# One core, chunked attention into a gated MLP: a weight load in two, one half's transposes on another engine, and output banks turned by two

## The chip, the cores and the metric

The kernel runs on one core of a Trainium2 chip. The metric is the device time of that core in microseconds (us), median of several executions. TensorE is called PE, its weight loads PEld, VectorE DVE, ScalarE ACT, GpSimd POOL, and SP issues most of the loads and stores (156 of the 159 DMA issues in the profile of before). "L702" is line 702 of the kernel. In the changed kernel every line that matters here has a number higher by one (L702 became L703).

## The reference

Two stages. The first is attention inside chunks of 64 positions, the second an MLP with a gate on all 4608 tokens:

```python
# q, k, v: (8, 8, 576, 64), 9 chunks of 64 per sequence
scores = np.matmul(q_c, k_c.transpose(0, 1, 2, 4, 3)) / np.sqrt(64)
attn = np.exp(scores - scores.max(-1, keepdims=True))
attn = attn / (attn.sum(-1, keepdims=True) + 1e-09)
x = np.matmul(attn, v_c)              # rearranged to (4608, 512)
h = x @ w_in                          # w_in  (512, 2048)
g = h / (1.0 + np.exp(-beta * h))
out = g @ w_out                       # w_out (2048, 512)
```

All inputs and the output are float32.

## The kernel before

The tokens go through in 9 blocks of 512, each of two **halves** h (h = 0 to 17). For each half the kernel casts q and k to bf16, turns them (transposes), makes the scores, the exponentials, the average of v, and turns the result into xT. For each block, `mm1` makes 16 tiles of x @ w_in, `gate` makes g from each, and `mm2` makes out. The kernel gives PE eight buffers for its results, the **banks**; it lets a bank be written again when the engine that reads it is done (in the trace of before, PE stands 1.31 us for a gate that reads its bank). A Python list scheduler fixes the order on each engine when the program is built: where several pieces of work are ready, the one of lowest rank goes first, by cost estimates in us. Each engine is given its list; in the trace of before, DVE, waiting for one entry, holds up the ready ones behind it (it stands 1.98 us, and a gate is ready for the last 0.9 of them).

```python
A0, A1, A2, A3, F3, F0, F1, F2 = range(8)     # the eight PSUM banks
FS = (F0, F1, F2, F3)

def load_w_in(j, queue):                      # piece j: 512 of 2048 columns, 1 MB
    ...
    P.dma(queue, (0.65, 32, 79), lambda e: e.dma_start(
        stage, w_in[:, f0:f0 + n].rearrange("(c p) f -> p c f", p=128)), ...)

def turn_pe(h, which, j, m, n):               # on PE, into a bank; 8 transposes for q, 8 for k
    ...
def keep_turned(h, which, j, m, n, eng):      # the copy out of that bank, q on ACT, k on DVE
    ...
def turn_dve(h, which, hb):                   # on DVE, 32-bit stream transpose, from SBUF to SBUF
    ...
def scores(h, cps, b=A0, first=0.2):          # after turn_pe: 32 matmuls
    ...
def scores_halved(h, first=0.2):              # after turn_dve: 64 smaller matmuls
    ...
def gate(blk, t, n, halves=(0, 1)):           # the DVE part is the one that frees the bank
    P.op("act", ..., lambda e: e.activation(tt[:, T % 3, c], bank(n)[:, c], AF.Tanh, scale=beta_half[:, t:t + 1]), ...)
    P.op("dve", ..., lambda e: e.scalar_tensor_tensor(
        g2[:, sg, t, c], tt[:, T % 3, c], 1.0, bank(n)[:, c], ALU.add, ALU.mult), ...)
...
PAIRED = (3, 4, 5)                            # halves turned on DVE; 0 to 2 on PE, 6 and later by DMA
HOLD = {(5, 0, 0): (1, 1)}                    # a turn_dve of half 5 waits for a gate of block 1

def turn(h, banks=(A0, A1)):
    for w in (1, 0):
        if h >= 2 and h not in PAIRED:
            go(r, cast_qk, h, w, 0, 8, "pool")
            go(r, turn_pe, h, w, 0, 8, banks[w])
            go(URGE.get(h, 0), keep_turned, h, w, 0, 8, banks[w], ("act", "dve")[w])
            continue
        if h >= 2:
            go(r, cast_rows, h, w, "pool")
            for hb in range(2):
                go(TD.get(h, 2), turn_dve, h, w, hb, after=gated.get(HOLD.get((h, w, hb))))
            continue
        ...
...
for j in range(4):
    for s in range(4):                        # block 0, second product: banks F0 to F3
        go(200 + 10 * j + s, mm2, 0, s, range(4 * j, 4 * j + 4), FS[s])
...
for t in range(4, 16):                        # block 1, first product
    ...
    go(300 + 4 * t, mm1, 1, t, FS[t % 4], hvs)
    gated[1, t] = go(0, gate, 1, t, FS[t % 4], hvs)
...
for blk in range(2, NB):                      # blocks 2 to 8: mm1 beside mm2 of the block before
    ...
        n = FS[i % 2]                         # mm1 in F0, F1
        m = FS[2 + s % 2] if 2 * blk + 2 < FIRST else F2   # mm2 in F2, F3
```

The softmax here doesn't subtract the row's maximum and nothing guards it: scores larger than these inputs give would overflow.

## Time and profile before

| what | before |
|---|---|
| device time, median of 3 | 294.1 us (293.81 to 294.6) |
| span of the profiled run | 292.8 us |
| PE busy | 277.7 us (95%) |
| DVE, ACT, POOL busy | 157.8, 149.3, 103.0 us |
| DMA share, 4 to 74 us | 1.04 to 1.16 |

PE is the bound. The lines that carry this are in the prediction below. One row of the table of stretches belongs here. The columns are the stretch and its length in us, then for PE, PEld, DVE, ACT and POOL the busy us with the number of instructions, then the granted PE clock, the DMA share and GB/s:

```profile
46.00:60.00 14.00, 12.49 (x252) 7.38 (x254) 8.51 (x17) 8.08 (x15) 8.90 (x12) 1.00 1.09 297
```

PE is busy 12.49 of 14 us here.

A warning for reading this profile: it lacks 34 matmul records of L730 (x558), while all 592 of its weight loads are there. Small gaps on the matmul row of before, such as "L730 <- issue", are partly these holes.

### The profile page before, as it was taken

How to read it: one execution, taken by the hardware profiler on the slowest of the kernel's cores; microseconds unless marked ns; L12 is line 12 of the kernel's file. 1: busy time of each engine (PE TensorE's matmuls, PEld its weight loads, DVE VectorE, ACT ScalarE, POOL GpSimd, SP SyncE). 2: the span in 40 equal slices, each digit the busy share in tenths (PEclk: the TensorE clock that was granted, in tenths of full speed). 3: DMA queues.
4: the chain of work that ended last, by engine and by line, in shares of the span. 5: the costliest groups of instructions: out<-in, count | busy, mean ns of one | idle time of the engine just before them, and what ended most of it. 6: DMA issues, size and time to landing. Idle time of an engine off the chain costs nothing.

```text
span 292.8 us, 6026 instructions
## 1 busy us (share of the span) xinstructions
PE 277.7 (95%) x2534; PEld 138.3 (47%) x2568; DVE 157.8 (54%) x280; ACT 149.3 (51%) x226; POOL 103.0 (35%) x112
## 2 busy tenths in 40 slices
PE   1999999899999999999999999999999999999995
PEld 1774444544444444444444444444444444444444
DVE  1557974798365355465655565655555544334300
ACT  3569533576555544545555555555555454454311
POOL 1444756535786845433243565212120000000000
PEclk9979999999999999999999999999999999999999
DMA  7999999999999999999898979282824110101133
GB/s 200 298 386 401 280 392 263 303 296 247 202 262 210 229 245 187 271 217 234 214 256 214 241 209 262 61 183 52 185 50 128 36 72 0 74 8 63 54 87 77
DMA packets 91722, 55.97 MB, mean 191 GB/s; under 512 B 76712, under 2 KB 76976, under 8 KB 91696
## 3 DMA queue, kind: packets, MB, share of 16 engines
q1 hardware_dynamic: 91520, 55.46, 73.6%
q8 instruction: 20, 0.33, 0.5%
q10 hardware_dynamic: 176, 0.14, 0.2%
q14 instruction: 6, 0.05, 0.0%
HBM read 36.71 MB, written 9.44 MB: 158 GB/s over the span
## 4 chain that ended last, share of the span: by engine, by line
PE 77%; DMA 11%; SPq 4%; DVE 3%; issue 1%; ACT 1%; POOL 1%; ACTq 0%; POOLq 0%
PE A L730 37%; PE A L702 37%; DMA qkstage<-in_moe_w_out_dram 5%; DMA g<-in_moe_w_out_dram 3%; DMA qkstage<-in_k_dram 3%; SPq L417 2%; PE A L615 2%; DVE g L720 2%; SPq L452 2%; PE A L566 1%; DVE w_out_bf L349 1%; SPq L432 1%; ACT tt L717 1%; POOL w_out_bf L349 1%; DVE qkO L522 0%
## 5 line engine op out<-in xcount | busy, mean ns | idle before, releaser
L720 DVE SCALAR_TENSOR_TENSOR g<-tt,A 128x512 bf16<-128x512 bf16 x144 | 97.4, 685 | 92.1 <-ACT tt L717 91.2
L717 ACT ACTIVATE tt<-A,beta_half 128x512 bf16<-128x512 f32 x144 | 98.4, 687 | 94.4 <-PE A L702 91.4
L702 PE MATMUL A<-xT,w_in_bf 128*128 128x512 bf16 (+1 forms) x608 | 142.5, 371 | 1.6 <-DVE g L720 1.6
L730 PE MATMUL A<-w_out_bf,g 128*128 128x512 bf16 (+1 forms) x558 | 135.6, 373 | 2.9 <-issue 0.8
L702 PEld LDWEIGHTS A<-xT,w_in_bf 128*128 128x128 bf16 x608 | 58.0, 99 | 64.6 <-DVE g L720 7.1
L730 PEld LDWEIGHTS A<-w_out_bf,g 128*128 128x128 bf16 x592 | 56.8, 98 | 64.4 <-POOL w_out_bf L349 0.6
L349 POOL COPY qkO<-qkT 128x1024 bf16<-128x1024 bf16 x17 | 33.4, 1980 | 31.7 <-DMA qkT<-qkb 31.7
L349 POOL CAST qkb<-qkstage 128x1024 bf16<-128x1024 f32 (+1 forms) x30 | 30.7, 1022 | 36.8 <-DMA qkstage<-in_k_dram 26.5
L347 ACT ACTIVATE ostage<-A 128x512 f32<-128x512 f32 (+1 forms) x36 | 21.3, 591 | 20.2 <-PE A L730 20.2
L349 POOL CAST v_bf<-vstage 128x512 bf16<-128x512 f32 x32 | 19.6, 615 | 20.5 <-DMA vstage<-in_v_dram 20.0
L655 DVE TENSOR_TENSOR xn<-A,R 128x512 bf16<-128x512 f32 (+2 forms) x44 | 25.4, 593 | 1.2
L603 ACT ACTIVATE E<-A 128x1024 bf16<-128x1024 f32 (+1 forms) x18 | 15.5, 880 | 4.8 <-PE A L566 4.1
L349 DVE COPY qkO<-qkT 128x512 bf16<-128x512 bf16 x14 | 11.3, 849 | 0.2 <-DMA qkT<-qkb 0.2
L503 PE MATMUL A<-ident,qkb 128*128 128x128 bf16 x48 | 4.6, 251 | 6.1 <-DVE qkb L349 5.7
L615 PEld LDWEIGHTS A<-v_bf,E 64*64 64x64 bf16 x576 | 6.9, 107 | 7.1 <-issue 4.2
L522 DVE STREAM_TRANSPOSE qkO<-qkb 128x256 uint32<-128x256 uint32 x12 | 6.9, 644 | 5.4 <-POOL qkb L349 5.4
L615 PE MATMUL A<-v_bf,E 64*64 64x65 bf16 x576 | 9.8, 195 | 0.0
L660 DVE RECIPROCAL R<-A 128x8 f32<-128x8 f32 (+2 forms) x36 | 7.2, 199 | 4.3 <-PE A L615 4.3
L349 POOL CAST w_in_bf<-wstage 128x512 bf16<-128x512 f32 (+1 forms) x10 | 5.8, 616 | 7.3 <-DMA wstage<-in_moe_w_in_dram 7.3
L744 DVE TENSOR_SCALAR ostage<-A 128x256 f32<-128x256 f32 x1 | 0.4, 425 | 13.3 <-PE A L730 13.3
L349 POOL CAST qkb<-wstage 128x1024 bf16<-128x1024 f32 x4 | 4.5, 1136 | 8.0 <-DMA wstage<-in_k_dram 5.5
L566 PE MATMUL A<-qkO 64*64 64x64 bf16 x480 | 7.0, 197 | 0.1
(36 smaller groups left out, 72.8 us busy)
## 6 DMA issues: line engine op xcount, KB each, us to landing
qkstage<-in_k_dram SPq DMA_DIRECT2D x16, 512.0 KB, 4.7
qkstage<-in_q_dram SPq DMA_DIRECT2D x16, 512.0 KB, 5.7
vstage<-in_v_dram SPq DMA_DIRECT2D x32, 256.0 KB, 6.6
out_dram<-ostage SPq DMA_DIRECT2D x16, 512.0 KB, 4.3
wstage<-in_moe_w_in_dram SPq DMA_DIRECT2D x4, 1024.0 KB, 8.6
qkstage<-in_moe_w_out_dram SPq DMA_DIRECT2D x2, 1024.0 KB, 15.7
g<-in_moe_w_out_dram SPq DMA_DIRECT2D x2, 1024.0 KB, 8.1
wstage<-in_q_dram SPq DMA_DIRECT2D x8, 128.0 KB
```

The costliest lines, as they stand in the source:

```text
L347: P.op("act", us, lambda e: e.activation(dst, src, AF.Copy, **kw), reads, writes)
L349: P.op(eng, us, lambda e: e.tensor_copy(dst, src), reads, writes)
L522: P.op("dve", 0.1 + 2.05e-3 * 256, lambda e: e.transpose(dst, qkb[:, s, which, 4 * hb:4 * hb + 4, :].rearrange("p a x -> p (a x)").bitcast ...
L566: return e.matmul(bank(b + hb)[64 * c2:64 * c2 + 64, 64 * i:64 * i + 64], qkO[r, s, 1, hp, 64 * c:64 * c + 64], qkO[r, s, 0, hp, 64 * c:64 ...
L603: P.op("act", act_us(128 * (b - a)), lambda e: e.activation(E[:, s, :, a:b, :].rearrange("p g i q -> p g (i q)"), S[:, :, 64 * a:64 * b], ...
L615: return e.matmul(bank(n)[64 * y:64 * y + 64, 65 * j:65 * j + 65], E[r, s, hb, 4 * cp + hp, :], v_bf[r, sv, 2 * hv + cp, 2 * hp + hb, 0:65])
L655: P.op("dve", 0.15 + 1.05e-3 * n, lambda e: e.tensor_tensor(dst, o[..., 0:64], r.unsqueeze(len(r.shape)).to_broadcast(shape), ALU.mult), r ...
L660: P.op("dve", 0.22, lambda e: e.reciprocal(r, o[..., 64]), reads=[K("ps", b, v=("o", h)) for b in banks], writes=[K("R", banks[0], v=h)])
L702: return e.matmul(bank(n)[:, c].rearrange("p (x t) -> p x t", t=64), w_in_bf[:, kt, 256 * m:256 * m + 256].rearrange("p (x t) -> p t x", t ...
L717: P.op("act", 0.075 + act_us(N), lambda e: e.activation(tt[:, T % 3, c], bank(n)[:, c], AF.Tanh, scale=beta_half[:, t:t + 1]), reads=[K("p ...
L720: P.op("dve", dve_us(N), lambda e: e.scalar_tensor_tensor(g2[:, sg, t, c], tt[:, T % 3, c], 1.0, bank(n)[:, c], ALU.add, ALU.mult), reads= ...
L730: P.op("pe", 0.2158 * (b - a) / 512, lambda e, t=t: e.matmul(bank(n)[:, 0:b - a], g2[:, sg, t, rows], w_out_bf[:, t, a:b], start=(t == 0), ...
```

## The change

Five parts, all in the first 75 us:

1. The first w_in piece is loaded in two halves of 512 KB, and its first four casts all go to POOL.
2. DVE's casts of w_in pieces 2 and 3 go behind gates of block 0 (WAITS).
3. Half 4's four DVE transposes are held behind half 3's normalization (HOLD with the value 3). The entries of HOLD for half 5 have no effect while half 5 is on PE.
4. Half 5 is turned on PE: PAIRED is (3, 4).
5. The banks of block 0's second and block 1's first product are turned by two (ROT). XD names the engines that were used already, so it changes nothing.

```diff
-        def load_w_in(j, queue):
+        def load_w_in(j, queue, xs=(0, 1)):
             ...
+            a, b = 256 * xs[0], 256 * xs[-1] + 256
+            P.dma(queue, (0.65, 32, (44, 79)[len(xs) - 1]), lambda e: e.dma_start(
+                stage[:, :, a:b], w_in[:, f0 + a:f0 + b].rearrange("(c p) f -> p c f", p=128)), ...)
 ...
-        FIRST_CASTS = (("pool", "act", "dve", "pool"), ("act", "pool", "act", "pool"))
-        PAIRED = (3, 4, 5)
+        FIRST_CASTS = (("pool", "pool", "pool", "pool"), ("pool", "act", "pool", "act"))
+        PAIRED = (3, 4)
         TD = {2: -2, 3: 0}
-        HOLD = {(5, 0, 0): (1, 1)}
+        SPLIT = 1
+        ROT = 2
+        XD = (1, 2, 3, 4, 5)
+        WAITS = {2: 0, 3: 5}
+        HOLD = {(4, 1, 0): 3, (4, 1, 1): 3, (4, 0, 0): 3, (4, 0, 1): 3, (5, 1, 0): (1, 1), (5, 1, 1): (1, 3),
+                (5, 0, 0): (1, 5), (5, 0, 1): (1, 7)}
 ...
         for j in range(4):
-            load(load_w_in, j, "sp")
+            for xs in ((0,), (1,)) if j < SPLIT else ((0, 1),):
+                load(load_w_in, j, "sp", xs)
 ...
         for t in range(4, 16):
+            if t % 4 == 0 and t > 4:
+                cast_piece(t // 4, gated.get((0, WAITS.get(t // 4))))
 ...
-                go(200 + 10 * j + s, mm2, 0, s, range(4 * j, 4 * j + 4), FS[s])
+                go(200 + 10 * j + s, mm2, 0, s, range(4 * j, 4 * j + 4), FS[(s + ROT) % 4])
 ...
-            go(300 + 4 * t, mm1, 1, t, FS[t % 4], hvs)
-            gated[1, t] = go(0, gate, 1, t, FS[t % 4], hvs)
+            go(300 + 4 * t, mm1, 1, t, FS[(t + ROT) % 4], hvs)
+            gated[1, t] = go(0, gate, 1, t, FS[(t + ROT) % 4], hvs)
```

More of the change, by code (lines that the diff above doesn't have):

```diff
@@ L447, in stage_w_in @@
                 [("wst", s, x, c, hb) for x in range(2) for c in range(4) for hb in range(2)]
-        def load_w_in(j, queue):
+        def load_w_in(j, queue, xs=(0, 1)):
             s, f0, n = PIECES[j]
             stage, names = stage_w_in(j)
-            P.dma(queue, (0.65, 32, 79), lambda e: e.dma_start(
-                stage, w_in[:, f0:f0 + n].rearrange("(c p) f -> p c f", p=128)),
-                writes=keys(names, ("in", j)))
+            a, b = 256 * xs[0], 256 * xs[-1] + 256
+            P.dma(queue, (0.65, 32, (44, 79)[len(xs) - 1]), lambda e: e.dma_start(
+                stage[:, :, a:b], w_in[:, f0 + a:f0 + b].rearrange("(c p) f -> p c f", p=128)),
+                writes=keys([n for n in names if n[2] in xs], ("in", j)))
         def cast_w_in(j, c0, c1, eng, xs=(0, 1)):
@@ L460, in cast_w_in @@
             cast(eng, (b - a) * (c1 - c0), w_in_bf[:, c0:c1, f0 + a:f0 + b], stage[:, c0:c1, a:b],
-                 keys(names, ("in", j)), [K("w_in", j, c, x) for c in range(c0, c1) for x in xs])
+                 keys([n for n in names if n[2] in xs], ("in", j)), [K("w_in", j, c, x) for c in range(c0, c1) for x in xs])
         def stage_w_out(j):
@@ L783, in bass_chunk_attention__then__act_swish_beta_kernel @@
         loads = [0]
-        gated, kept = {}, {}
+        gated, kept, normal = {}, {}, {}
         ORDER = (("w", 0), ("w", 1), ("qv", 2), ("w", 2))
@@ L811, in rank_of, with hold @@
             return -1000 + 10 * h
+        def hold(*what):
+            x = HOLD.get(what)
+            return normal[x] if isinstance(x, int) else gated.get(x)
         def turn(h, banks=(A0, A1)):
@@ L823, in turn @@
                     for hb in range(2):
-                        go(TD.get(h, 2), turn_dve, h, w, hb, after=gated.get(HOLD.get((h, w, hb))))
+                        go(TD.get(h, 2), turn_dve, h, w, hb, after=hold(h, w, hb))
                     continue
@@ L846, in average @@
             for cp in range(2):
-                go(URGE.get(h, 0), normalize, h, cp, after=kept["q"] if h == 0 else None)
+                normal[h] = go(URGE.get(h, 0), normalize, h, cp, after=kept["q"] if h == 0 else None)
                 go(-985 if h == 0 else r, turn_x_pe, h, cp, banks[cp])
-                kept[h] = go(URGE.get(h, -5 if (h, cp) == (0, 1) else 0), keep_x, h, cp, banks[cp], ("act", "dve")[cp if h else 0])
+                kept[h] = go(URGE.get(h, -5 if (h, cp) == (0, 1) else 0), keep_x, h, cp, banks[cp], ("act", "dve")[cp if h in XD else 0])
         waiting = []
@@ L914, in bass_chunk_attention__then__act_swish_beta_kernel, with cast_piece @@
                 go(-3, cast_w_in, 0, c, c + 1, eng, (x,))
-        for j in range(1, 4):
+        def cast_piece(j, after):
             for c, eng in enumerate(("pool", "act", "pool", "dve")):
-                go(0, cast_w_in, j, c, c + 1, eng, after=kept[1] if eng == "dve" else None)
+                go(0, cast_w_in, j, c, c + 1, eng, after=after if eng == "dve" else None)
+        cast_piece(1, kept[1])
         for t in range(4):
@@ L921, in bass_chunk_attention__then__act_swish_beta_kernel @@
             go(10 * t + 1, mm1, 0, t, FS[t], (1,))
-            go(0, gate, 0, t, FS[t])
+            gated[0, t] = go(0, gate, 0, t, FS[t])
         for t in range(4, 16):
+            if t % 4 == 0 and t > 4:
+                cast_piece(t // 4, gated.get((0, WAITS.get(t // 4))))
             go(10 * t, mm1, 0, t, t % 4)
@@ L946, in bass_chunk_attention__then__act_swish_beta_kernel @@
             for s in range(4):
-                go(200 + 10 * j + s, mm2, 0, s, range(4 * j, 4 * j + 4), FS[s])
+                go(200 + 10 * j + s, mm2, 0, s, range(4 * j, 4 * j + 4), FS[(s + ROT) % 4])
         for s in range(4):
-            finish(0, s, FS[s])
+            finish(0, s, FS[(s + ROT) % 4])
         for t in range(16 - EARLY, 16):
-            go(280 + t, mm1, 1, t, FS[t % 4], (0,))
-            go(0, gate, 1, t, FS[t % 4], (0,))
+            go(280 + t, mm1, 1, t, FS[(t + ROT) % 4], (0,))
+            go(0, gate, 1, t, FS[(t + ROT) % 4], (0,))
         for t in range(4):
-            go(300 + t, mm1, 1, t, FS[t], (0,))
+            go(300 + t, mm1, 1, t, FS[(t + ROT) % 4], (0,))
         for t in range(4):
-            go(304 + t, mm1, 1, t, FS[t], (1,))
-            gated[1, t] = go(0, gate, 1, t, FS[t], after=None)
+            go(304 + t, mm1, 1, t, FS[(t + ROT) % 4], (1,))
+            gated[1, t] = go(0, gate, 1, t, FS[(t + ROT) % 4])
         for t in range(4, 16):
             hvs = (1,) if t >= 16 - EARLY else (0, 1)
-            go(300 + 4 * t, mm1, 1, t, FS[t % 4], hvs)
-            gated[1, t] = go(0, gate, 1, t, FS[t % 4], hvs)
+            go(300 + 4 * t, mm1, 1, t, FS[(t + ROT) % 4], hvs)
+            gated[1, t] = go(0, gate, 1, t, FS[(t + ROT) % 4], hvs)
         for h in (4, 5):
```

## The prediction

The sum came to 0.5 + 1.2 - 0.8 + 0.5 = 1.4 us gained, 292.7 us. The marked cuts are statements about the hardware that no trace or run of this case shows, and what rested on them. An allowance for what the split costs the loads, an estimate that no trace showed, is in the 17.3 us of item 1, with it item 3 counts 0.5, below the 0.7 that stands there.

> **What bounds the kernel now.** I read the page first: busy times, then the forty slices.
>
> ```profile
> PE 277.7 (95%) x2534; PEld 138.3 (47%) x2568; DVE 157.8 (54%) x280; ACT 149.3 (51%) x226; POOL 103.0 (35%) x112
> ...
> PE   1999999899999999999999999999999999999995
> ...
> PEclk9979999999999999999999999999999999999999
> DMA  7999999999999999999898979282824110101133
> ```
>
> TensorE (PE) is busy 277.7 of 292.8 us; no other engine is near it. So only three things can shorten the run: less idle time on PE, less work on PE, or less of its work at a low clock. Then I asked who PE waited for, over the whole span. The columns are total us, times, longest:
>
> ```profile
> PE A L503 <- DVE qkb L349: 5.7, 1, 5.7
> PE A L702 <- DVE g L720: 1.6, 2, 1.3
> PE A L730 <- issue: 0.8, 5, 0.2
> PE A L681 <- DVE xn L655: 0.6, 2, 0.4
> PE A L730 <- DVE R L660: 0.5, 1, 0.5
> ```
>
> The 5.7 us is the first load at the start, which the change does not touch. The two waits of L702 (first MLP product) for L720 (gate on VectorE) and the one of L730 (second product) are what a reordering can win: 1.6 + 0.5 = 2.1 us. The table of stretches places them: PE idles 0.27 us in 17 to 30 us, 0.27 in 30 to 46, 1.51 in 46 to 60, 0.55 in 60 to 74, and only 0.32 in 74 to 100. After 74 us PE is full and the change alters nothing.
>
> The timeline of the stretch with the large wait names its cause:
>
> ```profile
> 56.24 1.14 DVE L522 STREAM_TRANSPOSE qkO<-qkb 128x256 uint32<-128x256 uint32 x2 [1.98 <-POOL qkb L349]
> ...
> 57.22 1.27 DVE L720 SCALAR_TENSOR_TENSOR g<-tt,A 128x512 bf16<-128x512 bf16 x2
> ...
> 57.96 1.90 PE L702 MATMUL A<-xT,w_in_bf 128*128 128x512 bf16 x8 [1.31 <-DVE g L720]
> ```
>
> VectorE runs in order. It stands 1.98 us before half 5's transposes, until GpSimd's cast of k (55.16 to 56.20, itself waiting for its load) is done. The first two gates of block 1 queue behind, though ScalarE had started their tanh at 54.63 and one tile takes 0.69 us, so the first gate could have run from about 55.3. PE finds no free bank until 57.96.
>
> The other place is the first weights:
>
> ```profile
> 17.08 1.56 POOL L349 CAST w_in_bf<-wstage 128x256 bf16<-128x256 f32 x4 [2.12 <-DMA wstage<-in_moe_w_in_dram]
> ...
> 17.94 1.06 PE L702 MATMUL A<-xT,w_in_bf 128*128 128x256 bf16 x4
> ```
>
> and the table of stretches of 1 us:
>
> ```profile
> 17.00:18.00 1.00, 1.00 (x9) 0.64 1.04 381
> 18.00:19.00 1.00, 1.00 (x7) 0.50 1.05 387
> 19.00:20.00 1.00, 1.00 (x8) 0.50 1.05 389
> ```
>
> The casts wait for the whole 1 MB piece (landed about 17.05). PE's first useful MLP matmuls start at 17.94, and four of 256 columns take 1.06 us there. The table's columns are the stretch, its length, PE busy and count, granted clock, DMA share, GB/s: the clock is halved from about 17.3 to 20.7.
>
> [...] the dip lasts about 3.4 us. [...] The trace shows the price: half 2, turned on PE, needs two copies out (1.02 us ACT, 1.21 us VectorE); half 5 on VectorE needs none, but four instructions of 0.64 us. [...]
>
> **The change, part by part.**
>
> 1. *First w_in piece in two loads.* The last v load lands about 14.35 and piece 0 at 17.05, so it streams some 2.7 us; half of it should be there at about 15.7. GpSimd now does all four casts of the first half, 0.39 us each (1.56 for four): 15.7 to 17.3. xT of half 0 is done at 15.69 + 1.24 = 16.93. So PE's first mm1 starts at 17.0 to 17.2 in place of 17.94: about 0.9 us earlier, mostly at half clock, so worth 0.45 to 0.9; I take 0.6. The second half lands about 17.3 [...], casts shared by GpSimd and ScalarE, ready by 18.1. [...]
>
> 2. *Casts of pieces 2 and 3 on VectorE behind gates.* Today VectorE waits 0.96 us for piece 3 at 26.66 with a gate ready, and PE then loses 0.27 us at 27.74. The new order puts that cast behind gate 5: +0.27.
>
> 3. *What caps 1 and 2.* The last w_out piece lands about 45.5. Its casts end at 46.4 to 47.2 (GpSimd) and PE starts on it at 47.45. Its tile 14 is ready at 47.18 and wanted about 47.9, so PE can arrive only 0.7 us earlier before it stands[...]. DMA share is above 1 throughout. Of the 0.87 I therefore count **0.5**.
>
> 4. *Half 4's transposes behind half 3's normalize.* VectorE does one 0.66 us transpose at 50.16 before half 3's reciprocal at 50.66. The swap brings half 3's xT forward some 0.7 us; half 4's transposes end near 54.5 as now (54.25). PE was busy meanwhile, so I count 0.
>
> 5. *Half 5 on TensorE.* VectorE loses four transposes (about 2.5 us) and the wait before them; it gains one copy of 1.21 us, ScalarE one of 1.02. Gate 0 of block 1 can run at 55.3 to 56.0, before PE wants its bank at 56.65: the stall of 1.31 us goes; I count **1.2**. PE pays: 16 transposes cost 1.07 us for half 2 (35.77), while the scores go from 64 small matmuls in 0.71 us to 32 in 0.45. That is **-0.8**.
>
> 6. *Banks of block 1 turned by two.* Block 1's tiles 14 and 15 now end on F0 and F1; tiles 12 and 13 on F2 and F3. The next mm2 uses F2, which is then free two tiles earlier. That should take the 0.55 us wait at 71.21: **0.5**.
>
> Sum: 0.5 + 1.2 - 0.8 + 0.5 = 1.4 us gained, 294.1 - 1.4 = **292.7 us**.
>
> **The rivals.**
> - *The wait moves to PE.* [...] if half 5's turn is placed before its cast (ends 56.2 and 57.67), PE stands instead of VectorE. Against it: the turn uses banks A1 and A0, which half 4's average (normalized 62.6 to 64.4, last copy at 67.15) holds first, long after the casts. Were it so, 294 to 295.
> - *Half 5's chain gets longer and delays block 2.* Its scores now wait for a turn of q after half 4's last copy, plus 1.02 us of copy, about 2 us more than now. mm2 of block 1 can fill PE, with g ready, and half 4 should finish earlier when VectorE no longer stands. If fill fails, 1 to 2 us come back: 293.5 to 294.5.
> - *DMA bounds the first 47 us, so the split costs.* [...]
> - *The clock dip goes.* If an earlier start kept the clock up, half of 3.4 us, 1.7, comes on top: 291. [...]
>
> **Range and chances.** The ceiling is all of PE's idle time after 17 us (about 2.6) plus 0.9 at the start plus 1.7 of clock: some 5 us, below the 5.9 that 2% takes. A loss of 2% would need a new wait of over 6 us, on an engine with buffers in between. The runs of before spread over 0.8 us. Range 291.2 to 294.2; chances 0.02 faster, 0.96 same, 0.02 slower.
>
> **What would show it.** First mm1 near 17.1; the clock dip still there; no VectorE wait of 1.98 us and no PE wait of 1.31 near 57; 16 more transposes on PE for half 5 and its scores near 0.45 us; no wait of L730 near 70; PE standing at most 0.3 us for the last w_out casts near 46; and the start of block 2's mm1 (74.89 now) at about 73.5. The prediction is wrong if PE shows a new wait over 1 us for half 5's copies or for banks in 60 to 76 us, if the loads of w_out land over 0.5 us later, or if the gain at 74 us is lost again later to half 6 and 7's loads and DMA transposes.

## The result, and the profile after

| | before | after |
|---|---|---|
| device time, median of 6 | 293.94 us (293.77 to 294.6) | 293.11 us (292.55 to 293.41) |
| ratio | | 0.9967, 95% interval 0.9953 to 0.9981 |
| span of the profiled run | 292.8 us | 291.3 us |

A ratio is the mean time of one kernel's fast runs over that of the other's fast runs of the same rounds, so it is not quite the ratio of the medians. Here it says 0.97 us of 294; the medians differ by 0.83. The same program, run again on two other chips, gave 0.9943 and 0.9946 (below), which is 1.6 to 1.7 us. The mean of the three, 0.9952, is 1.4 us. The 95% interval of one group of runs is thus narrower than the scatter between groups: I take **0.2%, some 0.5 us, as what one group of runs can tell**. Smaller matters are read from traces alone, and said to be so. Before's profiled run took 294.54 us, the slow end of its runs, so the 1.5 us between the two spans is a little more than the difference of the times.

The profile after. First the busy times and the two rows of slices for PE:

```profile
PE 280.6 (96%) x2552; PEld 139.1 (48%) x2552; DVE 156.2 (54%) x276; ACT 149.1 (51%) x226; POOL 103.9 (36%) x114
...
PE   2899999999999999999999999999999999999995
...
PEclk9979999999999999999999999999999999999999
```

Then PE's waits after the first load (total, times, longest), from the waits over the whole span:

```profile
PE A L682 <- DVE xn L656: 0.6, 2, 0.4
...
PE A L703 <- DVE g L721: 0.3, 1, 0.3
PE A L731 <- POOL w_out_bf L349: 0.2, 1, 0.2
```

The 1.6 us of L702 for the gate has become 0.3, and the 0.5 us of L730 near 71 us is gone. (The matmul row puts that one down to DVE's reciprocal; but it lacks a record there, x7 of 8, and the row of weight loads shows at 70.98 a wait of 0.43 for the gate, which frees the bank.) New is 0.2 for w_out. The stretch shown above, now without a gap:

```profile
46.00:60.00 14.00, 14.00 (x269) 8.60 (x268) 9.03 (x17) 9.62 (x17) 8.61 (x12) 1.00 1.07 299
```

And the timeline at the place of the old stall:

```profile
54.63 1.88 DVE L721 SCALAR_TENSOR_TENSOR g<-tt,A 128x512 bf16<-128x512 bf16 x3 [0.99 <-ACT tt L718]
...
55.31 4.06 PE L703 MATMUL A<-xT,w_in_bf 128*128 128x256 bf16 x20
```

DVE runs the first gates of block 1 as soon as ScalarE has their tanh, and PE's row has no bracket: it waited for nobody.

**Where the time went.** To see it stage by stage I put the kernels on one scale. Every weight load was given the time of its matmul at full clock (0.216 us for 512 columns, 0.108 for 256, 0.056 for a transpose, about 0.012 for a small one; estimates from stretches at a granted clock of 1.00: four of 512 columns took 0.86 us, 110.22 to 111.08 in before, ten weight loads for 256 columns 1.08 at 53.12, 32 small matmuls 0.38 at 112.04, and eight transposes 0.45 at 64.46 in after), and these were summed in the order of the trace. At each sum, the table shows when before was there, and how much **earlier** another kernel's profiled run was (minus: later), in us:

```
before at  after  again  third | no_split no_h4hold h5_dve  best2 | only_rot only_h5 no_rot | extra_load
   17.81    0.44   0.55   0.73 |  -1.05     0.40     0.71   0.59 |  -1.25    -1.35   0.14 |   0.21
   27.74    0.88   0.54   0.99 |  -0.66     1.20     1.02   1.35 |  -0.93    -0.96  -0.18 |   0.61
   31.75    0.24  -0.26   0.06 |  -0.65     0.05     0.08   0.37 |  -0.93    -0.95  -0.17 |  -1.42
   50.25    0.33  -0.21   0.16 |  -0.55     0.06     0.18   0.38 |  -0.83    -0.85  -0.07 |  -1.40
   54.96    0.91   0.36   0.73 |   0.02     0.06     0.75   0.95 |  -0.44    -0.47   0.50 |  -0.82
   58.24    2.21   1.66   2.03 |   1.32     1.54     2.05   2.25 |   0.68     1.02   1.80 |   0.48
   71.03    2.89   2.34   2.71 |   2.00     2.22     2.55   2.75 |   1.07    -0.04   0.74 |   1.16
   79.32    2.96   2.41   2.78 |   2.07     2.30     1.49   3.04 |   1.07     0.11   0.38 |   1.23
   95.46    2.67   2.10   2.50 |   1.79     2.01     1.49   2.76 |   1.06     0.02   0.28 |   0.94
  168.36    2.63   2.25   2.64 |   1.80     2.16     0.77   2.80 |   1.21    -2.06  -2.08 |   1.01
  280.74    2.08   2.25   2.26 |   1.79     2.14     0.76   2.80 |   1.20    -2.09  -2.08 |   0.99
```

(From 71 us on, kernels with half 5 on PE have 0.59 us more such work in all, 269.02 against 268.43, so 0.59 must be taken off their last rows; h5_dve, best2 and only_rot need nothing taken off. For after: 2.08 - 0.59 = 1.49, the difference of the spans.)

Down the column of after: 0.33 from the start, still there at 50 us; +0.58 by 55 us; +1.30 at the old stall; +0.68 up to 71 us, where the bank wait was; -0.26 on the way from there to 168 us; -0.55 after that (near 173 us); and -0.59 for the added work. The experiments take these one by one.

### The profile page after: what moved, and what is told of

Same layout as the page of the kernel before. It is cut to its first block, busy times and chain, and to the rows that moved or that the text cites. A ratio compares the mean times of both kernels' runs of the same rounds, so it can differ in the third digit from the quotient of the medians.

```text
span 291.3 us, 6030 instructions
## 1 busy us (share of the span) xinstructions
PE 280.6 (96%) x2552; PEld 139.1 (48%) x2552; DVE 156.2 (54%) x276; ACT 149.1 (51%) x226; POOL 103.9 (36%) x114
## 4 chain that ended last, share of the span: by engine, by line
PE 87%; DMA 5%; SPq 4%; DVE 1%; POOL 1%; issue 0%; ACT 0%
PE A L731 42%; PE A L703 39%; DMA qkstage<-in_moe_w_out_dram 5%; PE A L616 2%; SPq L453 2%; PE A L567 2%; SPq L417 2%; SPq L432 1%; DVE qkO L349 1%; PE A L504 1%; PE A L682 1%; POOL w_out_bf L349 1%; DVE g L721 0%; PE A L587 0%; ACT tt L718 0%
## 5 line engine op out<-in xcount | busy, mean ns | idle before, releaser
L703 PE MATMUL A<-xT,w_in_bf 128*128 128x512 bf16 (+1 forms) x608 | 140.8, 370 | 0.3 <-DVE g L721 0.3
L731 PE MATMUL A<-w_out_bf,g 128*128 128x512 bf16 (+1 forms) x592 | 140.2, 374 | 0.3 <-POOL w_out_bf L349 0.2
L731 PEld LDWEIGHTS A<-w_out_bf,g 128*128 128x128 bf16 x592 | 56.2, 98 | 63.9 <-POOL w_out_bf L349 1.3
L347 ACT ACTIVATE ostage<-A 128x512 f32<-128x512 f32 (+1 forms) x36 | 21.3, 591 | 25.5 <-PE A L731 25.5
L604 ACT ACTIVATE E<-A 128x1024 bf16<-128x1024 f32 (+1 forms) x20 | 16.6, 850 | 4.7 <-PE A L567 3.9
L504 PE MATMUL A<-ident,qkb 128*128 128x128 bf16 x64 | 5.8, 243 | 6.2 <-DVE qkb L349 5.6
L349 POOL CAST w_in_bf<-wstage 128x256 bf16<-128x256 f32 (+1 forms) x12 | 6.2, 551 | 6.5 <-DMA wstage<-in_moe_w_in_dram 6.5
L504 PEld LDWEIGHTS A<-ident,qkb 128*128 128x128 bf16 x64 | 4.6, 110 | 7.2 <-DVE qkb L349 5.8
L567 PE MATMUL A<-qkO 64*64 64x64 bf16 x512 | 7.7, 198 | 0.1
L567 PEld LDWEIGHTS A<-qkO 64*64 64x64 bf16 x512 | 6.1, 109 | 3.4 <-POOL v_bf L349 1.3
```

Source lines behind the costliest of these rows:

```text
L347: P.op("act", us, lambda e: e.activation(dst, src, AF.Copy, **kw), reads, writes)
L349: P.op(eng, us, lambda e: e.tensor_copy(dst, src), reads, writes)
L504: P.op("pe", 0.056, lambda e, i=i: e.transpose(dst[:, i, :], qkb[:, s, which, i, :], ident[:, :]), reads=[K("qkb", s, which, i // 4, v=h), ...
L567: return e.matmul(bank(b + hb)[64 * c2:64 * c2 + 64, 64 * i:64 * i + 64], qkO[r, s, 1, hp, 64 * c:64 * c + 64], qkO[r, s, 0, hp, 64 * c:64 ...
L604: P.op("act", act_us(128 * (b - a)), lambda e: e.activation(E[:, s, :, a:b, :].rearrange("p g i q -> p g (i q)"), S[:, :, 64 * a:64 * b], ...
L703: return e.matmul(bank(n)[:, c].rearrange("p (x t) -> p x t", t=64), w_in_bf[:, kt, 256 * m:256 * m + 256].rearrange("p (x t) -> p t x", t ...
```

## The experiments

The theory from the prediction: part 4 (half 5 off DVE) removes the stall, part 5 removes a bank wait, the start is capped by w_out's loads, part 3 is worth nothing. The rivals: it is the order on DVE and not the engine that removes the stall; the parts are not a sum but need each other; the start is the larger share. Twelve runs on three chips (called A, B, C), each beside runs of before on the same chip; before took 294.43, 294.44 and 293.96 us there.

| label | chip | median us | ratio to before, 95% |
|---|---|---|---|
| no_split | A | 292.75 | 0.9939 (0.9922 to 0.9956) |
| no_h4hold | A | 293.41 | 0.9965 (0.9948 to 0.9983) |
| h5_dve | A | 293.95 | 0.9987 (0.9965 to 1.0008) |
| no_rot | A | 295.9 | 1.0056 (1.0038 to 1.0073) |
| after_again | B | 292.74 | 0.9943 (0.9931 to 0.9956) |
| no_split2 | B | 293.57 | 0.9977 (0.9957 to 0.9997) |
| best1 | B | 293.55 | 0.9964 (0.9932 to 0.9996) |
| extra_load | B | 294.24 | 1.001 (0.9984 to 1.0036) |
| only_h5 | C | 297.26 | 1.0092 (1.0049 to 1.0135) |
| only_rot | C | 293.79 | 0.9976 (0.9938 to 1.0014) |
| best2 | C | 292.76 | 0.9945 (0.99 to 0.999) |
| after_third | C | 293.05 | 0.9946 (0.9907 to 0.9986) |

### The start: without the split, and one load more

no_split (and no_split2, the same program on chip B), against after:

```diff
-        FIRST_CASTS = (("pool", "pool", "pool", "pool"), ("pool", "act", "pool", "act"))
+        FIRST_CASTS = (("pool", "act", "dve", "pool"), ("act", "pool", "act", "pool"))
-        SPLIT = 1
+        SPLIT = 0
```

> The changed kernel with the first w_in piece in one load and its old cast engines; everything else as changed. Theory 'TensorE counts': the earlier first MLP matmul (17.43 in place of 17.94) is worth its 0.5 us, so the ratio to before goes from 0.9967 to about 0.9985 (293.5 us). Theory 'the load stream counts': the w_out pieces land at the same time, TensorE is held there and the time stays within 0.2 us of the changed kernel (ratio about 0.997); in the profile the position of half 3's scores (46.48 us) moves by less than 0.2 us[...].

> The kernel without the split load, again, now beside the changed kernel on one chip. Theory 'load stream': same time as the changed kernel within its interval (0.0015). Theory 'split costs': 0.002 to 0.003 below the changed kernel, as the two chips suggested (0.9939 against 0.9967). Theory 'TensorE counts': 0.002 above it.

after_again is the changed kernel with a comment added, on chip B:

> The changed kernel itself, to stand beside the others on one chip. Ratio to before 0.995 to 0.998 as on the first chip (0.9967); first MLP matmul at 17 to 17.5 us; the casts of the first and last w_out pieces start at 29.0 to 29.3 and 45.2 to 45.6 us as in all six profiles so far.

The split does its first job. In after's timeline:

```profile
15.77 1.44 POOL L349 CAST w_in_bf<-wstage 128x256 bf16<-128x256 f32 x4 [0.87 <-DMA wstage<-in_moe_w_in_dram]
...
17.43 1.06 PE L703 MATMUL A<-xT,w_in_bf 128*128 128x256 bf16 x4
...
18.30 0.75 POOL L349 CAST w_in_bf<-wstage 128x256 bf16<-128x256 f32 x2 [1.09 <-DMA wstage<-in_moe_w_in_dram]
```

The first half has landed at 15.77 and PE starts its first MLP product at 17.43. It does not always come so early: in two of the eight profiles of split kernels (no_rot and extra_load) the casts of the first half start only at 17.04 and 16.97. Without the split the piece had landed at 18.18 (no_split) and 17.99 (no_split2), and no_split's PE starts at 18.88. The 17.05 us of before's own profile was an early one. At 27.7 us after is 0.88 ahead of before, no_split 0.66 behind.

Then most of it goes. At 31.7 us the lead of after is 0.24, and its repeats stand at -0.26 and 0.06. The lines at that place in after:

```profile
29.01 1.62 POOL L349 CAST w_out_bf<-qkstage 128x512 bf16<-128x512 f32 x2 [1.38 <-DMA qkstage<-in_moe_w_out_dram]
...
29.94 1.36 PE L731 MATMUL A<-w_out_bf,g 128*128 128x512 bf16 x4 [0.16 <-POOL w_out_bf L349]
```

The matmul row shows a wait of only 0.16 us. The row of weight loads shows more:

```profile
29.93 0.12 PEld L731 LDWEIGHTS A<-w_out_bf,g 128*128 128x128 bf16 x2 [0.65 <-POOL w_out_bf L349]
...
30.68 0.12 PEld L731 LDWEIGHTS A<-w_out_bf,g 128*128 128x128 bf16 x2 [0.63 <-POOL w_out_bf L349]
```

Before's weight loads wait 0.16 and 0.47 us at this place, so after waits 0.65 us more: that is the lead that it loses (0.88 to 0.24). POOL starts the first w_out casts when that load has landed, and PE stands for them. The start of these casts lies between 28.70 and 29.50 us in all 13 profiles of kernels that leave the amount loaded as it is, split or not. To show that this load stream is the cap, extra_load puts one useless 512 KB load behind the w_in loads, into a buffer that nobody reads until later; every engine's order stays the same:

```diff
-                load(load_w_in, j, "sp", xs)
+                load(load_w_in, j, "sp", xs) if (j, xs) != (3, (0, 1)) else (load(load_w_in, j, "sp", xs), load(load_extra, "sp"))
```

> The changed kernel with one useless load of 512 KB behind the w_in loads (into gate rows that are written later); every engine's order is the same but for that one load. Theory 'the load stream bounds TensorE up to the last w_out piece': all w_out casts, half 3's scores (46.48) and the end move by the time of the load, about 1.3 us (half of the 2.7 us that a 1 MB piece takes), so 294.3 us, ratio 1.001. Theory 'TensorE bounds': the loads move by 1.3 us, the end by less than 0.4.

```profile
30.67 1.61 POOL L349 CAST w_out_bf<-qkstage 128x512 bf16<-128x512 f32 x2 [2.60 <-DMA qkstage<-in_moe_w_out_dram]
...
31.60 1.35 PE L731 MATMUL A<-w_out_bf,g 128*128 128x512 bf16 x4 [1.55 <-POOL w_out_bf L349]
```

The casts start 1.17 us later than in after_again (29.50), PE's wait grows from 0.31 to 1.55, and the time by 1.50 us on the same chip (294.24 against 292.74). For a PE that comes early, the stream of loads sets when it passes 30 us. So a start that is 0.9 us earlier than in before's profile can't be worth 0.9.

What the split is worth in time is not settled. On chip B the split kernel is 0.34% faster than no_split2, 0.8 us; but no_split on chip A has the best ratio of all. I leave it at 0 to 0.8 us. The traces say more than the comparison with before's one early profile: in the five other profiles without the split the casts start at 18.02 to 18.51, PE comes to the first w_out product at 30.97 to 31.68 and finds its casts done, and at 31.7 us those I placed on the scale stand at -0.65 to -0.95 (no_split, only_rot, only_h5). Against that usual landing, the split kernels (extra_load left out) are earlier there by some 0.4 to 1.3 us (after and no_rot, which have the same clock dip, by 0.5 to 1.2); how much of it is left in the time is not shown. Part 2 (the casts behind gates) was not run alone either: DVE's wait of 0.96 us before piece 3 is gone in after's trace, and with it PE's 0.27; but after_again and no_h4hold show a PE wait of 0.26 and 0.28 for a gate at that place, and what PE wins there ends in the same wait for w_out.

**The clock dip.** The prediction gave it up as a rival that would not come. It came in most runs. Of the 45 runs of kernels with the split, 8 have a mean clock of 0.994 or less (one dip as in before's trace, 17.3 to 20.7 us at a granted clock of 0.50, is 3.4 / 2 / 292 = 0.6%); of the 63 runs without the split (the 33 of before on chips A to C included), 40 have. The profile of after happened to have a dip; that of after_third has none, as the stretches of 1 us show:

```profile
18.00:19.00 1.00, 1.00 (x12) 0.90 (x10) 0.42 (x1) 0.23 (x1) 0.00 (x0) 1.00 1.05 389
19.00:20.00 1.00, 1.00 (x11) 0.90 (x10) 0.00 (x0) 0.00 (x0) 0.00 (x0) 1.00 1.05 389
```

Yet after_third is no earlier than after at 31.7 us (0.06 against 0.24): the quick PE came sooner to the loads and waited there, 0.88 us at 22.04 for casts of w_in and 0.68 at 30.35 for casts of w_out, where after shows 0 and 0.16. Over all 108 runs, each taken against the mean of its kernel and chip, a clock lower by one dip goes with 0.33 us more (95%: some 0.1 to 0.55), not with 1.7. That is a correlation in the records, not an experiment on the dip.

### Half 4's transposes not held

```diff
-        HOLD = {(4, 1, 0): 3, (4, 1, 1): 3, (4, 0, 0): 3, (4, 0, 1): 3, (5, 1, 0): (1, 1), (5, 1, 1): (1, 3),
+        HOLD = {(5, 1, 0): (1, 1), (5, 1, 1): (1, 3),
```

> The changed kernel without holding half 4's transposes behind half 3's normalize; the order differs in a dozen lines only, near 50 us. The prediction counted 0 for it: ratio stays 0.9967. Theory now, from comparing positions in the two traces: TensorE gained about 0.4 to 0.6 us between 50 and 55 us by it, so the ratio becomes 0.998 to 0.9987 (293.4 to 293.6 us), and an idle stretch or lower density shows on TensorE near 52 us.

The trace disagrees with "worth nothing". Between 50 and 55 us the lead of no_h4hold stays at 0.06, while after, after_again and after_third, with the hold, each gain 0.57 to 0.58. The wait that it removes stands on the row of weight loads, where I had not looked. In before's timeline:

```profile
51.60 0.23 PEld L681 LDWEIGHTS A<-ident,xn 128*128 128x128 bf16 x4 [0.53 <-DVE xn L655]
...
52.44 0.23 PEld L681 LDWEIGHTS A<-ident,xn 128*128 128x128 bf16 x4 [0.28 <-DVE xn L655]
```

and in after's:

```profile
50.86 0.43 PEld L682 LDWEIGHTS A<-ident,xn 128*128 128x128 bf16 x4
```

In these transposes of half 3's x it is the weight load that waits for DVE's xn; the matmul row, whose ends are modelled, shows no gap. no_h4hold has the same two waits back, 0.53 at 51.54 and 0.28 at 52.38. Some of the gain is given back at once: no_h4hold gains 1.48 at the old stall where after gains 1.30. In the time the part can't be seen: 0.9965 lies inside the spread of after's own three ratios.

### Half 5 back on DVE, behind gates

```diff
-        PAIRED = (3, 4)
+        PAIRED = (3, 4, 5)
```

This also brings to life the HOLD entries of half 5: its transposes now wait for gates 1, 3, 5 and 7 of block 1.

> The changed kernel with half 5 turned on VectorE again, but each of its four transposes held behind gate 1, 3, 5, 7 of block 1. Theory 'order': what removed the 1.31 us wait is that no transpose stands ahead of the first gates, not the engine; then the wait near 57 us stays away, TensorE saves the 16 transposes (0.6 us) and the time is about 292.5 us (ratio 0.995). Theory 'engine': VectorE stands for half 5's casts again; a wait of 0.5 us or more of the first product for a gate comes back in 54 to 66 us and the time is 293.5 or more.

The stall at 57 us stays away: h5_dve gains 1.30 there, just what after gains. So **the order on DVE is enough to remove the stall; the move to PE is not needed for it**. (The move alone does it too: only_h5, below, gains 1.49 there.) In best2, which also has half 5 on DVE (last experiment), three gates stand ahead of the first transpose:

```profile
54.58 1.88 DVE L721 SCALAR_TENSOR_TENSOR g<-tt,A 128x512 bf16<-128x512 bf16 x3 [1.00 <-ACT tt L718]
56.38 0.66 DVE L523 STREAM_TRANSPOSE qkO<-qkb 128x256 uint32<-128x256 uint32 x1
```

But h5_dve loses 1.06 us again between 71 and 79 us, to a wait that after does not have, half 6's scores for POOL's reordering:

```profile
77.82 0.45 PE L567 MATMUL A<-qkO 64*64 64x64 bf16 x32 [1.00 <-POOL qkO L349]
```

and 0.7 us more by 168 us, where PE waits at 151.92 for the copy-out of a result (0.69 us, 1.18 on the weight load). It ends at 0.9987.

### The banks, and half 5 alone

no_rot is after without the turned banks; only_h5 is before with half 5 on PE and nothing else; only_rot is before with the turned banks and nothing else:

```diff
no_rot:    -        ROT = 2
           +        ROT = 0
only_h5:   -        PAIRED = (3, 4, 5)
           +        PAIRED = (3, 4)
only_rot:  -                go(200 + 10 * j + s, mm2, 0, s, range(4 * j, 4 * j + 4), FS[s])
           +                go(200 + 10 * j + s, mm2, 0, s, range(4 * j, 4 * j + 4), FS[(s + ROT) % 4])
           ...  (and every FS[t % 4] of block 1 likewise, ROT = 2)
```

> The changed kernel with block 0's second product and block 1's banks not turned by two. Theory 'bank': the second product of block 1 must wait for the gate of tile 14 in place of tile 12; a wait of about 0.5 us shows near 68 us and the time is 293.6 (ratio 0.9985). Rival: half 5's later turn has already given the gates time; no wait, and the time is within 0.2 of the changed kernel, apart from what the other order of blocks 2 to 8 does.

> The kernel before with one part alone: half 5 on TensorE. Theory 'the parts need each other': the 1.31 us wait near 57 goes, but TensorE, with no second product ready, stands 1.0 to 1.5 us before half 5's scores (for ScalarE's copy of q, as without the turned banks) and has 0.6 us more to do; at the start of block 2 nothing is won or up to 1 us lost, and the time is 294 to 295.5 us (ratio 0.999 to 1.004). Theory 'sum of parts', as the prediction added them: 1.2 won less 0.8, ratio 0.9985.

> The kernel before with the turned banks alone. Sum of parts: the 0.55 us wait near 71 goes, ratio 0.998. Theory 'needs each other': the same 0.3 to 0.6 us here, not the 2 to 3 us that taking them out of the changed kernel cost; the wait of 1.3 us near 57 stays.

Alone, the turned banks do about what was predicted: only_rot gains 0.39 us between 58 and 71 us, and its time, 0.9976, can't be told from 1. (It also lost most of the stall at 57 us, 0.19 in place of 1.31, because in that profile PE came there later and POOL's cast earlier: the size of that stall moves from run to run.)

With half 5 on PE the banks matter more. Without them the timeline of no_rot shows

```profile
67.91 0.61 PE L504 MATMUL A<-ident,qkb 128*128 128x128 bf16 x8
69.91 0.45 PE L567 MATMUL A<-qkO 64*64 64x64 bf16 x32 [1.40 <-ACT qkO L347]
```

PE turns q, then stands 1.40 us until ScalarE has copied the result out; about 0.5 had been expected. only_h5 has the same wait of 1.40 at 70.70. In after there is work between the two:

```profile
67.50 0.61 PE L504 MATMUL A<-ident,qkb 128*128 128x128 bf16 x8
67.95 1.89 PE L731 MATMUL A<-w_out_bf,g 128*128 128x512 bf16 x8
69.77 0.45 PE L567 MATMUL A<-qkO 64*64 64x64 bf16 x32
```

The next mm2 writes bank F2. With ROT = 0, F2 held tile 14 of block 1 and must wait for its gate; with ROT = 2 it held tile 12. Eight second products, 1.89 us, then fit in the gap. This is the second rival of the prediction, "half 5's chain gets longer and delays block 2", and the turned banks are what keeps it away.

Between 79 and 168 us no_rot loses 2.46 us more and only_h5 2.17. Three waits that after doesn't have stand where it is lost: two of 0.7 us for the copy-out of results ("PE A L731 <- ACT ostage L347: 1.4, 2, 0.7" in no_rot; 1.18 each on the weight loads at 155.36 and 163.13), and one for the DMA that brings xT (0.62 at 134.73 in no_rot, 0.33 at 134.70 in only_h5). Both kernels have another order in blocks 2 to 8 from the scheduler; why it makes these copies late was not looked into.

In time: half 5 alone +0.92%, banks alone -0.24%, which add up to a loss; the change with both, and the other parts, gains 0.33 to 0.57%. The parts are not a sum. But the loss of half 5 alone, more than either theory expected, is not all the banks' doing. From 31.75 to 79.32 us only_h5 still wins 1.06 us, 0.47 after the added work; it loses 2.17 us to the other order behind that, and its late first load had cost 0.95. What the banks do with half 5 on PE is the difference up to 79.32 us: after wins 2.72 from 31.75 on, no_rot 0.55.

### Toward a better one, and the change a third time

best1 is no_split with half 5 on DVE; best2 is after with half 5 on DVE; both give half 6's scores twice the slack in the scheduler's view, so that other work is placed ahead of the wait for POOL that h5_dve showed:

```diff
-        PAIRED = (3, 4)
+        PAIRED = (3, 4, 5)
-                    go(r, scores, h, (0, 1), slack=SL)
+                    go(r, scores, h, (0, 1), slack=3.0 if h == 6 else SL)
```

> No split, half 5 on VectorE with its transposes behind gates 1, 3, 5, 7, and half 6's scores placed later (slack 3.0 in place of 1.5), since in the run before TensorE stood 1.0 us there for GpSimd's reordering. If that wait was what ate the 0.6 us of saved transposes, TensorE shows no wait over 0.5 us between 52 and 82 us and the time is 0.3 to 0.6 us below the kernel without the split (ratio 0.992 to 0.994). If another wait takes its place, the ratio stays above 0.995.

> The changed kernel (split kept) with half 5 on VectorE behind the gates 1, 3, 5, 7 and half 6's scores later. If the 1.0 us wait for GpSimd at half 6's scores was all that the version with half 5 on VectorE lost, TensorE shows no wait over 0.5 us from 46 to 82 us and the time is 0.4 to 0.6 us below the changed kernel on this chip (ratio about 0.993). Rival: the later order of blocks 2 to 8 gives it back; same as the changed kernel.

> The changed kernel a third time, as the neighbour of the three on this chip: ratio 0.994 to 0.997. How far it lies from its two other results shows how far the same program moves from submission to submission.

best1 had one run slow (297.69 us, left out of the ratio), and its others spread from 291.4 to 295.05; it is no better than after_again. best2 has the lowest span of any profile, 290.0 us. Its wait at 78 us is gone and nothing is lost after 71 us: 2.75 there, 2.80 at the end, with no extra work to take off. But its six runs, 291.71 to 293.75, lie across those of after_third on the same chip, 292.16 to 293.59, and the medians are 0.29 us apart. So nothing is shown to beat the change.

## Why the prediction was right or wrong

292.7 was predicted and 293.11 measured, with 292.74 and 293.05 on two other chips, all inside the range, and "within 2%" holds. The mean gain of the three comparisons, 1.4 us, is the predicted 1.4. The sum came out better than its terms, and that is partly luck. After's column adds up to 0.33 (start) + 0.58 (part 3) + 1.30 (stall) + 0.68 (up to 71 us) - 0.26 - 0.55 (later losses) - 0.59 (added work) = 1.49: part 3, counted as 0, and cheaper added work made up for a smaller start and for the 0.81 lost later, which was not foreseen.

- **The bound** was read rightly: PE, and then PE's idle time. The ceiling has a slip: its 2.6 us is PE's idle time from 17 to 74 us only, not all of it after 17; the stretches up to 291 us show 3.4 us more (some of it holes of the profile). The small chances outside 2% held all the same.
- **Parts 1 and 2, 0.5 us: the mechanism was right, the term too large.** The first half landed at 15.77 as said (15.7). The second landed at 18.27 and not 17.3 (17.03 to 18.81 over the six profiles of split kernels in which the first half came by 15.93; in the other two it came near 17.0). PE started at 17.43, not by 17.2. The cap by w_out's loads, step 3, was right in kind and came earlier: PE stood for the first w_out casts near 30 us, not the last ones near 46. What was left at 31.7 us is 0.24, -0.26 and 0.06 in three profiles. The rival "the split costs" is not borne out: no kernel without the split was earlier than before at 31.7 us.
- **The dip** was said to stay. It stayed in after's profile, but most runs of the split kernels have none. It did not hurt the sum: after_third, which has no dip, waited 0.88 and 0.68 us for the casts of the same loads.
- **Part 3 (the prediction's item 4), counted 0**, measured 0.57 us locally in three profiles. The step that failed is "PE was busy meanwhile": I read the matmul row, and the wait was 0.53 + 0.28 us on the row of weight loads.
- **The stall, 1.2 us:** it measured 1.30, against the one profile of before; only_rot, with the same order on DVE, stood only 0.19, so the gain in a usual run is not known. The reason was half right. DVE standing 1.98 us for POOL's cast ahead of ready gates was the cause; h5_dve shows that moving gates ahead cures it as well as moving the transposes away.
- **PE's work, -0.8 us: a bit too large.** The 16 transposes take 0.45 us each eight up to the next instruction (64.46 to 64.91 and 67.50 to 67.95), so 0.90 in all and not 1.07. The scores save 0.27 (0.64 to 0.37 by the starts of their successors). That is -0.63; the nominal work says -0.59.
- **The banks, 0.5 us:** alone 0.39, with half 5 on DVE 0.50 (h5_dve, best2). As a lone term it was right. What the sum hid is that with half 5 on PE this part also prevents the 1.40 us wait of the second rival. That rival was named, and answered with "mm2 of block 1 can fill PE"; I did not see that the fill is there only because of part 5.
- **After 74 us "the change alters nothing"** was wrong by 0.55 us in after: at 173 us PE waits 0.30 us for a gate (0.80 on the weight load) that queues behind two reorderings on DVE.

```profile
170.28 2.60 DVE L349 COPY qkO<-qkT 128x512 bf16<-128x512 bf16 x2
...
173.54 1.04 PE L703 MATMUL A<-xT,w_in_bf 128*128 128x512 bf16 x4 [0.30 <-DVE g L721]
```

The repeats lost 0 and 0.4 us over the same stretch, so it is partly the timing of one run; which part is the new order and which is chance stays open.

Of the signs listed: the DVE wait of 1.98 us and the L730 wait near 70 are gone as said, the transposes and scores are as said. Block 2's first mm1 stands at 76.27, where 73.5 was said; but by then after has done 16 more second products than before had, 16 x 0.216 = 3.5 us, so at equal work it is at 72.8.

## What to carry to other kernels

Look for waits on the row of weight loads as well as on the matmul row (here 0.53 + 0.28 us showed only there), and place two traces on a scale of work done, so that a gain can be followed until it is used up: here 0.64 of the 0.88 us won by 28 us was spent at 30 us, waiting for the next load. When work moves to the engine that is the bound, ask what that engine will do while the longer chain runs, and whether a free buffer lets it; the part that frees the buffer may decide how much of the other part's gain is kept. Before crediting an engine change, try the same cure by order alone.
